# First weights in two DMAs, wider matmuls for tiles 2 and 3, interleaved statistics, and 1/den by one DMA, in a linear-attention and GELU block on one core

## The chip, the cores and the metric

The kernel runs on one core of a Trainium2 chip. The metric is device time in microseconds (us), from repeated executions; the profile is one execution more. In the profile PE is TensorE, PEld its weight loads, DVE VectorE, ACT ScalarE, POOL GpSimd, SP the engine that issues most DMAs. L352 is line 352 of the kernel; since the change adds lines, L352 of before is L355 of after, and L615 is L622.

A rounded map of the run: 0 to 7 us loading and the first normalised tile; 7 to 60 us `h = gelu(xn W1)`; 60 to 127 us the attention projections; 127 to 205 us the output products, with the division by the attention's denominator on the way.

## The reference, cut to what matters

```python
xn = (x - mean) / sqrt(var + 1e-5)                 # x is 2048 x 640, bf16
q, k, v = split(xn @ wqkv)                         # 32 heads of 20
pq, pk = phi(q), phi(k)
num = pq @ (pk.T @ v)                              # per head
den = pq @ sum(pk) + 1e-6
out = x + (num / den) @ wo + (gelu(xn @ w1 + b1) @ w2 + b2)   # w1: 640 x 1536
```

## The kernel before

Tokens come in 16 tiles of 128; 640 is five blocks k of 128, and W1's 1536 columns are 12 column blocks (`JT`) of 128, loaded as four quarters of three blocks (`JQ` = 3). All DMAs but two are issued from SP, in this order.

```python
dma_x(0, 1)
dma_w("scalar", b1tmp[:], ...)            # issued from ScalarE
dma_w1(0, "scalar")                       # W1's first quarter, 480 KB, issued from ScalarE
dma_x(1, 1)
dma_w1(1)
dma_x(2, 1)
dma_w1(2)
dma_x(3, 1)
dma_w1(3)
# ... x 4-5, 6-7, 8-11, 12-15; the other weights are queued behind the transposes
```

A helper records each operation with what it reads and writes, and puts in the semaphore waits. A filler is a warm-up matmul whose result nobody reads. One unit of `h` is five matmuls and a GELU on ScalarE:

```python
def h_unit(t0, n, jb):                    # n tiles from t0, column block jb
    # five matmuls: W1[:, k, block jb] against xnT[:, k, n*128 tokens], then GELU + bias on ScalarE
def ln_next(t):
    if t + 1 < NT:
        ln_half(t + 1, 0)                 # half the statistics of the next tile, VectorE
        ln_half(t + 1, 1)
    ln_norm(t)                            # VectorE; waits for rstd(t) from GpSimd
    if t + 1 < NT:
        ln_aggr(t + 1)                    # VectorE aggregate, then GpSimd power -> rstd = 1/sqrt(var + eps)

filler(10)                                # warm-up matmuls, 512 wide
# ... tile 0 normalised in two parts, transposed on TensorE, copied to xnT
h_first([0, 1, 2])                        # tile 0, first quarter: k 0,1 for three blocks, then k 2..4
xnT_copy(1, transp(1))
ln_stats(2)
ln_next(2)
units(0, 1, 3, 2 * JQ)                    # tile 0, second quarter
units(1, 1, 0, 2 * JQ)
units(0, 2, 2 * JQ, 2 * JQ + 2)           # tiles 0 and 1 together, 256 wide
xnT_copy(2, transp(2))
units(0, 2, 2 * JQ + 2, JT)
ln_next(3)
ln_next(4)
units(2, 1, 0, JQ)
xnT_copy(3, transp(3))
units(2, 1, JQ, JT)                       # tile 2 alone, 128 wide
units(3, 1, 0, JT)                        # tile 3 alone, 128 wide
for t in range(4, NT):                    # tiles 4..15 are transposed by DMA
    if t > 4:
        ln_next(t)
    # SP: dma_start_transpose(xnT[:, :, tile t], xn_tm[:, t, :])
for (t0, n) in [(4, 2), (6, 2), (8, 4), (12, 4)]:
    units(t0, n, 0, JT)
```

The division: 1/den is 32 rows (heads) for a chunk of 512 tokens; four DMAs spread it to 128 partitions, and VectorE multiplies it into `PQ`.

```python
def rden_dma(c):
    for i in range(4):
        # SP: dma_start(rdb(c)[i:P:4, :], rden[H * c:H * (c + 1), :])
```

Of the kernel before, what the change touches and what calls it, by code (L numbers as in the profile page):

```python
# [6 lines left out]
ACT = mybir.ActivationFunctionType  # L7
P = 128
# [104 lines left out]
def bass_parallel_sum__linear_attn_block__dense_activation_gelu__prompt_kernel(  # L113
# [6 lines left out]
    CW = CH * P  # L120
    NC = NT // CH
    DT = D // P
    JT = F // P
    H = 32
# [5 lines left out]
    Pl = Planner(nc)  # L130
    R_ = Pl.res
# [5 lines left out]
    with contextlib.ExitStack() as es:  # L137
# [12 lines left out]
        W1 = W1f[:].rearrange("p (k f) -> p k f", k=DT)  # L150
# [25 lines left out]
        rden = sb("rden", [P, CW], BF16)  # L176
# [3 lines left out]
        B_ = [R_("bank%d" % i) for i in range(8)]  # L180
# [22 lines left out]
        r_xn = [R_("xn%d" % t) for t in range(NT)]  # L203
        r_xnT = [R_("xnT%d" % t) for t in range(NT)]
        NW1 = 4
        r_W1 = [R_("W1_%d" % i) for i in range(NW1)]
        r_Wq, r_Wk, r_Wv, r_W2, r_Wo = R_("Wq"), R_("Wk"), R_("Wv"), R_("W2"), R_("Wo")
        r_b1tmp, r_b1c, r_b2 = R_("b1tmp"), R_("b1c"), R_("b2")
# [6 lines left out]
        r_PQ = [[R_("PQ%d_%d" % (c, j)) for j in range(DT)] for c in range(NC)]  # L215
# [5 lines left out]
        r_den, r_rden = R_("den"), R_("rden")  # L221
# [5 lines left out]
        def dma_x(t, n):  # L227
            src = xv[t * P:(t + n) * P, :].rearrange("(t p) d -> p t d", p=P)
            Pl.ins("sync", lambda e: e.dma_start(x_in[:, t:t + n, :], src),
                   writes=r_x[t:t + n], dma=True)  # L230

        def dma_w(eng, dst, src, res):
            Pl.ins(eng, lambda e: e.dma_start(dst, src), writes=[res], dma=True)  # L233

        w1v = B_w1.rearrange("(k p) n -> p k n", p=P)
        wqv = A_wqkv.rearrange("(k p) n -> p k n", p=P)
        FW = F // NW1
        def dma_w1(i, eng="sync"):
            dma_w(eng, W1[:, :, i * FW:(i + 1) * FW], w1v[:, :, i * FW:(i + 1) * FW], r_W1[i])
        dma_x(0, 1)  # L240
        dma_w("scalar", b1tmp[:], B_b1.rearrange("(a p) -> a p", p=P), r_b1tmp)
        dma_w1(0, "scalar")
        dma_x(1, 1)
        dma_w1(1)
        dma_x(2, 1)
        dma_w1(2)
        dma_x(3, 1)
        dma_w1(3)
        dma_x(4, 2)
        dma_x(6, 2)  # L250
        for c in range(2, NC):
# [10 lines left out]
        v = "vector"  # L262
# [7 lines left out]
               reads=[r_ident], writes=[r_ident])  # L270
# [22 lines left out]
        def filler(n):  # L293
            b = take(1)
            Pl.ins("tensor", [lambda e: e.matmul(bank(b), warm[:, 0:P], warm[:], start=True, stop=True)
                              for _ in range(n)], reads=[r_warm], writes=[B_[b]])

        def b1_step():
            b = take(1)
            Pl.ins("tensor", lambda e: e.transpose(bank(b).bitcast(BF16)[:, 0:JT], b1tmp[:], ident[:JT, :JT]),  # L300
                   reads=[r_b1tmp, r_ident], writes=[B_[b]])
            Pl.ins("scalar", lambda e: e.activation(b1c[:], bank(b).bitcast(BF16)[:, 0:JT], ACT.Copy),
                   reads=[B_[b]], writes=[r_b1c])


        def ln_half(t, h):
            s = t % 4
            Pl.ins(v, lambda e: e.bn_stats(stats[:, s, 6 * h:6 * h + 6], x_in[:, t, h * HW:(h + 1) * HW]),  # L308
                   reads=[r_x[t]], writes=[r_stats[s][h]])
            if h == 0:  # L310
                Pl.ins(g, lambda e: e.tensor_single_scalar(stats[:, s, 2:3], stats[:, s, 2:3], D * EPS, ALU.add),
                       reads=[r_stats[s][0]], writes=[r_stats[s][0]])

        def ln_aggr(t):
            s = t % 4
            Pl.ins(v, lambda e: e.bn_aggr(aggr[:, s, :], stats[:, s, :]),  # L316
                   reads=r_stats[s], writes=[r_aggr[s]])
            Pl.ins(g, lambda e: e.tensor_tensor(out=rstd[:, s:s + 1], in0=aggr[:, s, 1:2],  # L318
                                                in1=mhalf[:], op=ALU.pow),
                   reads=[r_aggr[s], r_small], writes=[r_rstd[s]])  # L320

        def ln_stats(t):
            ln_half(t, 0)
            ln_half(t, 1)
            ln_aggr(t)

        def ln_norm(t):
            s = t % 4
            Pl.ins(v, lambda e: e.tensor_scalar(xn_tm[:, t, :], x_in[:, t, :], aggr[:, s, 0:1], rstd[:, s:s + 1],
                                                ALU.subtract, ALU.mult),  # L330
                   reads=[r_x[t], r_aggr[s], r_rstd[s]], writes=[r_xn[t]])
# [32 lines left out]
        def norm0(lo, hi, res):  # L364
            Pl.ins(v, lambda e: e.tensor_scalar(xn_tm[:, 0, lo:hi], x_in[:, 0, lo:hi], aggr[:, 0, 0:1], rstd[:, 0:1],
                                                ALU.subtract, ALU.mult),
                   reads=[r_x[0], r_aggr[0], r_rstd[0]], writes=[res, r_xn[0]])

        def transp0(k0, k1, res):
            b = take(1)  # L370
            pT = bank(b).bitcast(BF16)
            Pl.ins("tensor", [(lambda e, k=k: e.transpose(pT[:, (k - k0) * P:(k - k0 + 1) * P],
                                                          xn_tm[:, 0, k * P:(k + 1) * P], ident[:]))
                              for k in range(k0, k1)],
                   reads=[res, r_ident], writes=[B_[b]])
            return xnT[:, k0:k1, 0:P], pT[:, 0:(k1 - k0) * P].rearrange("p (k q) -> p k q", k=k1 - k0), b

        def h_first(jbs):
            bs = [take(1) for _ in jbs]
            for (ks, res) in (((0, 1), r_xnTA), ((2, 3, 4), r_xnT[0])):  # L380
                for jb, b in zip(jbs, bs):
                    Pl.ins("tensor", [(lambda e, k=k, jb=jb, b=b: e.matmul(  # L382
                        bank(b, 0, P), W1[:, k, jb * P:(jb + 1) * P], xnT[:, k, 0:P],
                        start=(k == 0), stop=(k == DT - 1))) for k in ks],
                        reads=[r_W1[jb * P // FW], res], writes=[B_[b]])
            for jb, b in zip(jbs, bs):
                Pl.ins("scalar", lambda e, jb=jb, b=b: e.activation(
                    HG[:, jb, 0:P], bank(b, 0, P), ACT.Gelu_apprx_tanh, bias=b1c[:, jb:jb + 1]),
                    reads=[B_[b], r_b1c], writes=[r_HG[0][jb]])

        r_xnTA = R_("xnT0A")
        Pl.ins("scalar", lambda e: e.activation(b1c[:, 0:1], warm[:, 0:1], ACT.Gelu_apprx_tanh),
               reads=[r_warm], writes=[r_b1c])
        filler(10)
        ln_stats(0)
        ln_half(1, 0)
        ln_half(1, 1)
        ln_aggr(1)
        norm0(0, CA, r_xnA)
        norm0(CA, D, r_xnB)  # L400
        dA, sA, bA = transp0(0, 2, r_xnA)
        filler(1)
        dB, sB, bB = transp0(2, DT, r_xnB)
        Pl.ins(v, lambda e: e.tensor_copy(dA, sA), reads=[B_[bA]], writes=[r_xnTA])
        Pl.ins("scalar", lambda e: e.activation(dB, sB, ACT.Copy), reads=[B_[bB]], writes=[r_xnT[0]])
        b1_step()
        ln_norm(1)
        h_first([0, 1, 2])

# [5 lines left out]
        def units(t0, n, lo, hi):  # L415
            for jb in range(lo, hi):
                h_unit(t0, n, jb)

        def ln_next(t):
            if t + 1 < NT:  # L420
                ln_half(t + 1, 0)
                ln_half(t + 1, 1)
            ln_norm(t)
            if t + 1 < NT:
                ln_aggr(t + 1)

        xnT_copy(1, transp(1))
        ln_stats(2)
        ln_next(2)
        units(0, 1, 3, 2 * JQ)  # L430
        units(1, 1, 0, 2 * JQ)
        units(0, 2, 2 * JQ, 2 * JQ + 2)
        xnT_copy(2, transp(2))
        units(0, 2, 2 * JQ + 2, JT)
        ln_next(3)
        ln_next(4)
        units(2, 1, 0, JQ)
        xnT_copy(3, transp(3))
        units(2, 1, JQ, JT)
        units(3, 1, 0, JT)  # L440
        for t in range(TD, NT):
            if t > TD:
                ln_next(t)
# [128 lines left out]
        def rden_scale(c):  # L572
            cc = slice(c * CW, (c + 1) * CW)
            for j in range(DT):
                Pl.ins(v, lambda e, j=j: e.tensor_tensor(out=PQ[:, j, cc], in0=PQ[:, j, cc], in1=rdb(c), op=ALU.mult),
                       reads=r_rdb[c] + [r_PQ[c][j]], writes=[r_PQ[c][j]])

        ekf = ek[:].rearrange("p a d -> p (a d)")
        r_rdb = [[R_("rdb%d_%d" % (c, i)) for i in range(4)] for c in range(NC)]

        def rdb(c):
            return ekf[:, c % 3 * CW:(c % 3 + 1) * CW]

        def rden_dma(c):
            for i in range(4):
                Pl.ins("sync", lambda e, i=i: e.dma_start(rdb(c)[i:P:4, :], rden[H * c:H * (c + 1), :]),
                       reads=[r_rden], writes=[r_rdb[c][i]] + ([r_rdb[0][i]] if c == 3 else []), dma=True)

        def x_again(c):
            src = xv[c * CW:(c + 1) * CW, :].rearrange("(t p) d -> p t d", p=P)  # L590
# [133 lines left out]
```

## Time and profile before

| | before |
|---|---|
| time, median of 3 runs | 208.4 us (207.85 to 208.42) |
| span of the profiled execution | 206.8 us |
| TensorE busy | 98% |
| first real matmul | 6.87 us |
| fourth column block of tile 0 | 8.04 us |

The page's first line, its busy shares and its chain of what ended last:

```profile
span 206.8 us, 3962 instructions
...
PE 203.2 (98%) x1588; PEld 140.3 (68%) x1588; DVE 112.3 (54%) x231; ACT 73.1 (35%) x141; POOL 21.1 (10%) x59
...
PE 96%; DMA 3%; ACTq 0%; DVE 0%; issue 0%
```

The chain in order of time (start, length, what):

```profile
1.45 5.37 DMA W<-in_B_w_dram
6.82 0.05 issue
6.87 1.01 PE ps L382 x15
7.88 0.28 PE ps L336 x5
8.16 3.65 PE ps L352 x55
...
60.35 21.73 PE ps L473 x160
```

One DMA (W1's first quarter) holds the start back; then TensorE works to the end. So a change pays only by starting this stream sooner or by making it shorter. (The chain uses modelled ends of matmuls; L352's first matmul starts at 8.04.)

Two rows of the timeline, from the answers for 0 to 22 and 22 to 42 us (start, length, engine, line, operation, shape, count):

```profile
15.33 6.90 PE L352 MATMUL ps<-xnT,W 128*128 128x128 bf16 x113
...
21.74 20.49 PE L352 MATMUL ps<-xnT,W 128*128 128x256 bf16 x151
```

A row merges neighbours of one line and tile and shows the shape of the first. The program has 105 matmuls of 128 columns there, not 113, so the first row ends inside the 256-wide ones, and the second's start is only the edge of the window asked for. I overlooked that; narrower windows, asked after the result, show one shape each:

```profile
15.83 4.35 PE L352 MATMUL ps<-xnT,W 128*128 128x128 bf16 x75
...
22.83 10.43 PE L352 MATMUL ps<-xnT,W 128*128 128x256 bf16 x94
```

Taking off the last matmul's own length (0.219 and 0.273 us), that is (4.35 - 0.219)/74 = 55.8 ns a matmul at 128 columns and (10.43 - 0.273)/93 = 109.2 ns at 256.

VectorE's wait for 1/den in the list of waits (total, times, longest):

```profile
DVE PQ L575 <- DMA ek<-rden: 3.9, 1, 3.9
```

It is long, but no TensorE wait stands beside it: TensorE has products that need no division until 143.88 us.

### The profile page before, as it was taken

The page shows a single profiled execution, that of the slowest core. Times are in us where ns is not written, and L with a number is a line of the kernel's source. Part 1 is how long each engine was busy: PE and PEld are TensorE (multiplying, and loading weights), DVE is VectorE, ACT ScalarE, POOL GpSimd, SP SyncE. Part 2 cuts the span into 40 slices and gives each one's busy share as a digit, 9 for nine tenths or more (in the row PEclk, how much of TensorE's full clock was granted, in tenths as well). Part 3 has the DMA queues.
Part 4 walks back from the last instruction along what each step waited for, and adds up shares of the span by engine and source line. Part 5 has one row for each costly group of instructions (what it writes and reads, how often), then busy time and mean ns, then how long its engine had stood idle before and what let it go on. Part 6 is the DMA issues. An engine that isn't in the chain of part 4 may idle for free.

```text
span 206.8 us, 3962 instructions
## 1 busy us (share of the span) xinstructions
PE 203.2 (98%) x1588; PEld 140.3 (68%) x1588; DVE 112.3 (54%) x231; ACT 73.1 (35%) x141; POOL 21.1 (10%) x59
## 2 busy tenths in 40 slices
PE   7999999999999999999999999999999999999996
PEld 2799987444457777777756556677777777777775
DVE  4589970000007888999288888574863522522332
ACT  2689887666676555111153554400000000000000
POOL 3235568000022000000000000000000000000000
DMA  5999668998000000000300001931111111001002
GB/s 173 338 355 116 105 128 108 376 318 310 3 0 0 0 0 3 0 3 0 63 0 5 0 0 25 373 117 50 64 66 57 56 47 56 32 32 36 32 32 63
DMA packets 24043, 18.32 MB, mean 89 GB/s; under 512 B 10584, under 2 KB 24024, under 8 KB 24024
## 3 DMA queue, kind: packets, MB, share of 16 engines
q1 hardware_dynamic: 23344, 17.57, 29.8%
q10 hardware_dynamic: 680, 0.49, 0.9%
q8 instruction: 12, 0.20, 0.4%
q14 instruction: 7, 0.06, 0.1%
HBM read 12.62 MB, written 2.62 MB: 74 GB/s over the span
## 4 chain that ended last, share of the span: by engine, by line
PE 96%; DMA 3%; ACTq 0%; DVE 0%; issue 0%
PE ps L615 34%; PE ps L352 25%; PE ps L473 11%; PE ps L512 11%; PE ps L524 10%; DMA W<-in_B_w_dram 3%; PE ps L651 2%; PE ps L551 1%; PE ps L533 1%; PE ps L562 1%; PE ps L382 0%; PE ps L336 0%; ACTq L233 0%; DVE out_sb L654 0%
## 5 line engine op out<-in xcount | busy, mean ns | idle before, releaser
L352 PE MATMUL ps<-xnT,W 128*128 128x128 bf16 (+2 forms) x435 | 52.0, 282 | 0.0
L615 PE MATMUL ps<-W,HG 128*128 128x320 bf16 x360 | 51.0, 299 | 0.0
L352 PEld LDWEIGHTS ps<-xnT,W 128*128 128x128 bf16 x435 | 35.5, 98 | 15.7
L615 PEld LDWEIGHTS ps<-W,HG 128*128 128x128 bf16 x360 | 35.1, 98 | 14.2 <-issue 0.4
L356 ACT ACTIVATE HG<-ps,b1c 128x128 bf16<-128x128 f32 (+2 forms) x87 | 40.0, 492 | 12.6 <-PE ps L352 10.4
L634 DVE TENSOR_TENSOR out_sb<-ps,xnT 128x640 bf16<-128x640 f32 x15 | 12.4, 825 | 33.8 <-PE ps L615 33.6
L460 ACT ACTIVATE ek<-ps 128x512 bf16<-128x512 f32 (+1 forms) x36 | 23.2, 644 | 20.3 <-PE ps L524 11.1
L461 DVE TENSOR_SCALAR ek<-ek 128x512 bf16<-128x512 bf16 (+1 forms) x36 | 10.9, 304 | 33.7 <-ACT ek L460 32.6
L615 PE MATMUL ps<-Msb,PQ 128*128 128x320 bf16 x150 | 22.3, 299 | 0.0
L524 PE MATMUL ps<-xnT,Wqkv 128*128 128x512 bf16 x100 | 21.9, 379 | 0.0
L473 PE MATMUL ps<-Wqkv,xnT 128*128 128x320 bf16 x160 | 21.9, 299 | 0.0
L512 PE MATMUL ps<-xPK,xn_tm 128*128 128x320 bf16 x160 | 21.9, 299 | 0.0
L473 PEld LDWEIGHTS ps<-Wqkv,xnT 128*128 128x128 bf16 x160 | 15.7, 98 | 6.2
L512 PEld LDWEIGHTS ps<-xPK,xn_tm 128*128 128x128 bf16 x160 | 15.7, 98 | 6.1
L615 PEld LDWEIGHTS ps<-Msb,PQ 128*128 128x128 bf16 x150 | 14.7, 98 | 5.7
L524 PEld LDWEIGHTS ps<-xnT,Wqkv 128*128 128x128 bf16 x100 | 11.7, 118 | 9.5
L308 DVE BATCH_NORM_STATS2 stats<-xPK 128x6 f32<-128x320 bf16 x32 | 13.6, 466 | 2.8 <-DMA xPK<-in_A_x_dram 2.7
L463 DVE SCALAR_TENSOR_TENSOR PQ<-ps,ek 128x512 bf16<-128x512 f32 x20 | 13.8, 692 | 2.1
L463 DVE SCALAR_TENSOR_TENSOR xPK<-ps,ek 128x640 bf16<-128x640 f32 x16 | 13.2, 825 | 1.7
L499 DVE TENSOR_TENSOR Msb<-Msb,xPK 128x640 f32<-128x640 f32 x14 | 11.6, 825 | 0.5
L318 POOL TENSOR_TENSOR rstd<-aggr,mhalf 128x1 f32<-128x1 f32 x16 | 9.1, 568 | 8.9 <-DVE aggr L316 8.9
L516 ACT ACTIVATE W<-ps 128x640 bf16<-128x640 f32 x5 | 3.5, 703 | 18.2 <-PE ps L512 18.2
(61 smaller groups left out, 93.4 us busy)
## 6 DMA issues: line engine op xcount, KB each, us to landing
xnT<-in_A_x_dram SPq DMA_DIRECT2D x4, 640.0 KB, 6.8
Wqkv<-in_A_wqkv_dram SPq DMA_DIRECT2D x3, 800.0 KB, 6.9
out_dram<-out_sb SPq DMA_DIRECT2D x15, 160.0 KB, 1.8
W<-in_B_w_dram SPq DMA_DIRECT2D x1, 1920.0 KB, 15.4
W<-in_B_w_dram SPq DMA_DIRECT2D x3, 480.0 KB, 7.2
xPK<-in_A_x_dram SPq DMA_DIRECT2D x2, 640.0 KB, 8.6
Wo<-in_A_wo_dram SPq DMA_DIRECT2D x1, 800.0 KB, 10.8
xPK<-in_A_x_dram SPq DMA_DIRECT2D x4, 160.0 KB, 4.3
```

Of the source, the lines that this page charges most:

```text
L308: Pl.ins(v, lambda e: e.bn_stats(stats[:, s, 6 * h:6 * h + 6], x_in[:, t, h * HW:(h + 1) * HW]), reads=[r_x[t]], writes=[r_stats[s][h]])
L352: Pl.ins("tensor", [(lambda e, k=k: e.matmul(bank(b, 0, w), W1[:, k, jb * P:(jb + 1) * P], xnT[:, k, tok], start=(k == 0), stop=(k == DT - ...
L356: Pl.ins("scalar", lambda e: e.activation(HG[:, jb, tok], bank(b, 0, w), ACT.Gelu_apprx_tanh, bias=b1c[:, jb:jb + 1]), reads=[B_[b], r_b1c ...
L460: Pl.ins("scalar", lambda e: e.activation(e2, src, ACT.Exp), reads=br, writes=[r_ek[s]])
L461: Pl.ins(v, lambda e: e.tensor_scalar(et, et, 1.0, 1e-6, ALU.min, ALU.add), reads=[r_ek[s]], writes=[r_ek[s]])
L463: Pl.ins(v, lambda e: e.scalar_tensor_tensor(out=d2, in0=src, scalar=0.0, in1=e2, op0=ALU.max, op1=ALU.add), reads=br + [r_ek[s]], writes= ...
L473: fns.append(lambda e, k=k, h=h, b=b, t=t: e.matmul(bank(b + h, 0, HW), xnT[:, k, t * P:(t + 1) * P], Wqkv[:, k, D + h * HW:D + (h + 1) * ...
L499: Pl.ins(v, lambda e, t=t: e.tensor_tensor(out=zsum, in0=zsum, in1=PK[:, t, :], op=ALU.add), reads=[r_PK[t], r_zsum], writes=[r_zsum])
L512: Pl.ins("tensor", [(lambda e, t=t, h=h, b=b, f=f: e.matmul(bank(b + h, 0, HW), xn_tm[:, t, f * P:(f + 1) * P], PK[:, t, h * HW:(h + 1) * ...
L524: Pl.ins("tensor", [(lambda e, k=k, j=j, b=b: e.matmul(bank(b), Wqkv[:, k, j:D:DT], xnT[:, k, cc], start=(k == 0), stop=(k == DT - 1))) fo ...
L615: return lambda e: e.matmul(bank(b + h, 0, HW), l, r[:, h * HW:(h + 1) * HW], start=(i == 0), stop=(i == JT + DT - 1))
L634: Pl.ins(v, lambda e: e.tensor_tensor(out=halves(out_sb[:, s, :]), in0=pair(b), in1=halves(x_res[:, t, :]), op=ALU.add), reads=B_[b:b + 2] ...
```

## The change

The intent: W1's first quarter comes by two DMAs on two queues, so that tile 0 can begin with k blocks 0 and 1; tile 0's norm goes ahead of tile 1's aggregate; tiles 2 and 3 share the second half of W1 at 256 wide; only half of the next tile's statistics precedes each norm; 1/den takes one DMA a chunk, its source repeated four times.

```diff
+        KA = 2
         dma_x(0, 1)
         dma_w("scalar", b1tmp[:], ...)
-        dma_w1(0, "scalar")
+        dma_w("scalar", W1[:, 0:KA, 0:FW], w1v[:, 0:KA, 0:FW], r_W1A)
         dma_x(1, 1)
+        dma_w("sync", W1[:, KA:DT, 0:FW], w1v[:, KA:DT, 0:FW], r_W1[0])
         dma_w1(1)
+        dma_w1(2)
         dma_x(2, 1)
-        dma_w1(2)
+        dma_w1(3)
         dma_x(3, 1)
-        dma_w1(3)
@@ start
-        filler(10)
+        filler(6)
+        b1_step()
+        filler(3)
         ln_stats(0)
         ln_half(1, 0)
         ln_half(1, 1)
-        ln_aggr(1)
         norm0(0, CA, r_xnA)
         norm0(CA, D, r_xnB)
+        ln_aggr(1)
   (the two copies of tile 0's transposes change places: part A on ScalarE, part B on VectorE)
@@ ln_next
                 ln_half(t + 1, 0)
-                ln_half(t + 1, 1)
             ln_norm(t)
             if t + 1 < NT:
+                ln_half(t + 1, 1)
                 ln_aggr(t + 1)
@@ order of the units
         xnT_copy(1, transp(1))
-        ln_stats(2)
-        ln_next(2)
         units(0, 1, 3, 2 * JQ)
         units(1, 1, 0, 2 * JQ)
-        units(0, 2, 2 * JQ, 2 * JQ + 2)
+        units(0, 2, 2 * JQ, 3 * JQ)
+        ln_stats(2)
+        ln_norm(2)
+        ln_stats(3)
+        units(0, 2, 3 * JQ, 3 * JQ + 1)
         xnT_copy(2, transp(2))
-        units(0, 2, 2 * JQ + 2, JT)
+        units(0, 2, 3 * JQ + 1, JT)
         ln_next(3)
-        ln_next(4)
         units(2, 1, 0, JQ)
         xnT_copy(3, transp(3))
-        units(2, 1, JQ, JT)
-        units(3, 1, 0, JT)
+        units(2, 1, JQ, 2 * JQ)
+        ln_next(4)
+        units(3, 1, 0, 2 * JQ)
+        units(2, 2, 2 * JQ, JT)
@@ 1/den
-            for i in range(4):
-                dma_start(rdb(c)[i:P:4, :], rden[H * c:H * (c + 1), :])
+            src = rden[H * c:H * (c + 1), :].unsqueeze(1).to_broadcast([H, 4, CW])
+            dma_start(rdb(c), src)
```

More of the change, by code (lines that the diff above doesn't have):

```diff
@@ L205, in bass_parallel_sum__linear_attn_block__dense_activation_gelu__prompt_kernel @@
         NW1 = 4
+        r_W1A = R_("W1_0A")
         r_W1 = [R_("W1_%d" % i) for i in range(NW1)]
@@ L384, in h_first @@
                         start=(k == 0), stop=(k == DT - 1))) for k in ks],
-                        reads=[r_W1[jb * P // FW], res], writes=[B_[b]])
+                        reads=[r_W1A if res is r_xnTA else r_W1[jb * P // FW], res], writes=[B_[b]])
             for jb, b in zip(jbs, bs):
@@ L403, in bass_parallel_sum__linear_attn_block__dense_activation_gelu__prompt_kernel @@
         dB, sB, bB = transp0(2, DT, r_xnB)
-        Pl.ins(v, lambda e: e.tensor_copy(dA, sA), reads=[B_[bA]], writes=[r_xnTA])
-        Pl.ins("scalar", lambda e: e.activation(dB, sB, ACT.Copy), reads=[B_[bB]], writes=[r_xnT[0]])
-        b1_step()
+        Pl.ins("scalar", lambda e: e.activation(dA, sA, ACT.Copy), reads=[B_[bA]], writes=[r_xnTA])
+        Pl.ins(v, lambda e: e.tensor_copy(dB, sB), reads=[B_[bB]], writes=[r_xnT[0]])
         ln_norm(1)
@@ L575, in rden_scale @@
                 Pl.ins(v, lambda e, j=j: e.tensor_tensor(out=PQ[:, j, cc], in0=PQ[:, j, cc], in1=rdb(c), op=ALU.mult),
-                       reads=r_rdb[c] + [r_PQ[c][j]], writes=[r_PQ[c][j]])
+                       reads=[r_rdb[c], r_PQ[c][j]], writes=[r_PQ[c][j]])
         ekf = ek[:].rearrange("p a d -> p (a d)")
-        r_rdb = [[R_("rdb%d_%d" % (c, i)) for i in range(4)] for c in range(NC)]
+        r_rdb = [R_("rdb%d" % c) for c in range(NC)]
         def rdb(c):
@@ L584, in rden_dma @@
         def rden_dma(c):
-            for i in range(4):
-                Pl.ins("sync", lambda e, i=i: e.dma_start(rdb(c)[i:P:4, :], rden[H * c:H * (c + 1), :]),
-                       reads=[r_rden], writes=[r_rdb[c][i]] + ([r_rdb[0][i]] if c == 3 else []), dma=True)
+            src = rden[H * c:H * (c + 1), :].unsqueeze(1).to_broadcast([H, 4, CW])
+            Pl.ins("sync", lambda e: e.dma_start(rdb(c), src),
+                   reads=[r_rden], writes=[r_rdb[c]] + ([r_rdb[0]] if c == 3 else []), dma=True)
         def x_again(c):
```

## The prediction

> **What bounds the kernel now.** The page gives TensorE 98% busy over a 206.8 us span; the chain of waits that ended last is 96% TensorE and 3% DMA. The DMA piece is W1's first quarter: issued 1.45 us, landed 6.82; the first 15 real matmuls start at 6.87. From there to 204.95 the chain is TensorE without a gap.
>
> **What the change does, costed from the trace.**
>
> 1. Tiles 2 and 3, second half of W1: 60 matmuls 128 wide become 30 of 256. The timeline shows 105 of 128 columns from 15.49 to 21.74 us (59.5 ns each) and 120 of 256 from 21.74 to about 34.6 (107 ns each). Saved: 60 x 59.5 - 30 x 107 = 0.36 us, all on the critical path.
>
> 2. W1's first quarter in two parts. By packet counts in the DMA view the first 192 KB lands at about 4.7 us, the rest near 6. Tile 0's norm becomes the first limit: rstd ends at 5.07, and the norm no longer waits for tile 1's aggregate (5.42 to about 5.18). Then transposes, ScalarE's copy (about 0.4 us, from 0.49 for 384 columns), VectorE's copy: first matmuls at about 6.25, ending about 7.35 instead of 7.88.
>
> 3. The next gate stops most of that. W1's second quarter, issued 1.72, took 6.3 us: it landed at 8.02, and its matmuls started at 8.04. The same bytes must still move ahead of it; the skill's "DMA: Bandwidth & Descriptors", section "Issuing engines are not separate DMA queues", says a second queue saves only sequencer time, and the DMA share is about 100% from 4 us on. I expect it at 7.7 to 8.1, TensorE idle 0.2 to 0.5 us before it, and a net gain of 0.1 to 0.3 us.
>
> 4. Half statistics: x2 lands about 1.5 us later (W1's third quarter goes ahead); tile 2's norm then ends at about 12.2 against a need at 12.9. In the steady loop one half (0.42 us) is left to hide rstd's latency (aggregate start to norm 0.96 us), so its period grows from 1.32 to about 1.75 us a tile. Tile 5's DMA transpose then lands at about 21.3, just when tiles 4 and 5 are wanted (about 21.4). Cost: 0 to 0.4 us.
>
> 5. 1/den by one DMA a chunk: VectorE waits 3.9 us for it and scales at 142.18, but TensorE has unscaled products until 143.88 and never waits. Three issues of 0.6 us go; landing moves to about 140.5. Worth nothing.
>
> **Sum.** -0.36 - 0.2 + 0.05 = about -0.5 us: 207.9 us. Eight in ten: 207.2 to 208.5. Before's three runs span 0.57 us. Faster by over 2%: 1%. Within 2%: 98.5%. Slower: 0.5%.
>
> **What the profile would show.** First real matmul at about 6.25 without a DMA wait; a wait for W1 before the fourth column block, at about 8.0; 60 fewer 128-wide matmuls, 30 more 256-wide; tiles 4 and 5's matmuls at about 21.3 rather than 21.74; late norms 1.75 us apart, the last at about 36 rather than 30; VectorE's wait for 1/den down to about 2 us; everything after 60 us the same, shifted.
>
> **What would make it wrong.** W1's second quarter landing clearly earlier (gain up to 0.9 us), or later[...]; tile 5's transpose late (TensorE idle before tiles 4 and 5); TensorE's clock, cold for the ten fillers (0.43 us each), warming later with the shorter filler run.

## More of the kernel before

The granted TensorE clock was 1.0 in all but three runs: two of the kernel before (210.12 and 210.41 us) at 0.992, and one of e6 at 0.999. The two of before raise its mean in the calls of e5 to e8 and of e9 to e12, so that the ratios there lean towards the edits and their intervals are wide.

## The result, and the profile after

| | before | after |
|---|---|---|
| time, median of 6 runs | 208.29 us (207.85 to 208.42) | 208.31 us (208.03 to 208.65) |
| ratio, 95% interval | | 1.0004 (0.9990 to 1.0018) |
| span of the profiled execution | 206.8 us | 207.0 us |
| first real matmul | 6.87 us | 6.38 us |
| W1's second quarter landed | 7.99 us | 8.17 us |
| fourth column block of tile 0 | 8.04 us | 8.21 us |
| tiles 4 and 5, first matmul | 21.19 us | 21.43 us |
| first matmul of the projections | 60.19 us | 60.43 us |

A ratio is the mean time of one kernel's runs over that of the other's runs of the same rounds, so it is not quite the ratio of the medians quoted. The landings and single matmul starts are read one by one from the trace.

The time did not change. The prediction's range held, but the gain of 0.5 us in it did not come.

```profile
span 207.0 us, 3868 instructions
...
PE 202.8 (98%) x1557; PEld 139.5 (67%) x1557; DVE 113.7 (55%) x231; ACT 72.7 (35%) x135; POOL 21.5 (10%) x59
...
PE 95%; DMA 3%; SPq 1%; issue 0%; DVE 0%
```

TensorE has 31 matmuls and 31 weight loads fewer (30 by widening, one warm-up). The chain of after:

```profile
2.20 5.96 DMA W<-in_B_w_dram
8.17 0.05 issue
8.21 4.87 PE ps L355 x65
...
15.57 5.79 PE ps L355 x75
21.36 0.07 issue
21.43 39.16 PE ps L355 x240
60.59 21.73 PE ps L480 x160
```

The DMA in the chain is now W1's *second* quarter. By single matmul starts the fourth block begins 0.17 us later than before (8.04 to 8.21). What the earlier first matmuls gained is a hole in front of it, named by the waits between 7 and 9 us:

```profile
PE ps L355 <- DMA W<-in_B_w_dram: 0.4, 1, 0.4
```

The second new interruption is at 21.36: "issue" there is a wait that the profile gives to nobody. The trace has 0.346 us between two matmul starts that are 0.109 apart elsewhere, so 0.24 us are lost, and the next matmul is the first of tiles 4 and 5. Tile 5's transpose, asked for alone:

```profile
L451 SPq DMA_TRANSPOSE xnT<-xn_tm x1: 1199/1199/1199, 18.8 to 18.8; - x1
...
DMA to landing us min/median/max: 2.5/2.5/2.5
```

It was issued at 18.80 and landed at 21.34; TensorE went on at 21.43. In before the same transpose was issued at 17.19 and landed at 19.76, ahead of the need at 21.19:

```profile
L444 SPq DMA_TRANSPOSE xnT<-xn_tm x1: 1203/1203/1203, 17.2 to 17.2; - x1
...
DMA to landing us min/median/max: 2.6/2.6/2.6
```

The sum of the two profiles: +0.17 (fourth block), then -0.17 from there to the end of tile 3 (before 21.19 - 8.04 = 13.15 us, after 21.19 - 8.21 = 12.98), then +0.24 (tile 5): +0.24, which is 60.43 - 60.19. The -0.17 holds 60 x 55.8 - 30 x 109.15 = 0.07 us of widening; before's wait of 0.08 us ahead of tile 2's transposes is gone too. Two profiles are two executions, though, and the timed runs are equal; how much a single one may wander is seen below.

VectorE's wait for 1/den fell, to 2.8 us where about 2 was predicted, with nothing in the chain changed there (66.12 us from 134 to 200 us in both):

```profile
DVE PQ L582 <- DMA ek<-rden: 2.8, 1, 2.8
```

### The profile page after: what moved, and what is told of

It is laid out like the page before. It is cut to its first block, busy times and chain, and to the rows that moved or that the text cites. A ratio compares the mean times of both kernels' runs of the same rounds, so it can differ in the third digit from the quotient of the medians. Undisturbed runs are those within 1.5% of the kernel's fastest.

```text
span 207.0 us, 3868 instructions
## 1 busy us (share of the span) xinstructions
PE 202.8 (98%) x1557; PEld 139.5 (67%) x1557; DVE 113.7 (55%) x231; ACT 72.7 (35%) x135; POOL 21.5 (10%) x59
## 4 chain that ended last, share of the span: by engine, by line
PE 95%; DMA 3%; SPq 1%; issue 0%; DVE 0%
PE ps L622 34%; PE ps L355 25%; PE ps L519 10%; PE ps L480 10%; PE ps L531 10%; DMA W<-in_B_w_dram 3%; PE ps L658 2%; PE ps L558 1%; PE ps L540 1%; PE ps L569 1%; SPq L230 0%; PE ps L339 0%; SPq L234 0%; DVE out_sb L661 0%
## 5 line engine op out<-in xcount | busy, mean ns | idle before, releaser
L355 PE MATMUL ps<-xnT,W 128*128 128x256 bf16 (+2 forms) x405 | 52.1, 290 | 0.5 <-DMA W<-in_B_w_dram 0.4
L359 ACT ACTIVATE HG<-ps,b1c 128x256 bf16<-128x256 f32 (+2 forms) x81 | 39.6, 510 | 13.7 <-PE ps L355 11.3
L467 ACT ACTIVATE ek<-ps 128x512 bf16<-128x512 f32 (+1 forms) x36 | 23.2, 645 | 20.3 <-PE ps L531 10.6
L311 DVE BATCH_NORM_STATS2 stats<-xPK 128x6 f32<-128x320 bf16 x32 | 14.7, 470 | 3.8 <-DMA xPK<-in_A_x_dram 3.8
```

Source lines behind the costliest of these rows:

```text
L311: Pl.ins(v, lambda e: e.bn_stats(stats[:, s, 6 * h:6 * h + 6], x_in[:, t, h * HW:(h + 1) * HW]), reads=[r_x[t]], writes=[r_stats[s][h]])
L355: Pl.ins("tensor", [(lambda e, k=k: e.matmul(bank(b, 0, w), W1[:, k, jb * P:(jb + 1) * P], xnT[:, k, tok], start=(k == 0), stop=(k == DT - ...
L359: Pl.ins("scalar", lambda e: e.activation(HG[:, jb, tok], bank(b, 0, w), ACT.Gelu_apprx_tanh, bias=b1c[:, jb:jb + 1]), reads=[B_[b], r_b1c ...
L467: Pl.ins("scalar", lambda e: e.activation(e2, src, ACT.Exp), reads=br, writes=[r_ek[s]])
```

## The experiments

My theory after the result: (1) widening is worth 0.07 us, not 0.36; (2) the start is held by W1's second quarter; (3) tile 5's transpose holds what is left; (4) 1/den is worth nothing. Rivals are named with each run. Below, a gate is an arrival that TensorE has to wait for: W1's second quarter is the first, tile 5's transpose the second. Four kernels went in five rounds, and "before" is the kernel before in the same rounds.

### e1_den: before with 1/den by one DMA alone

The edit is the last hunk of the change alone.

> The kernel before with nothing but 1/den by one DMA a chunk. My theory: worth nothing, ratio 0.999 to 1.001, because VectorE's wait for 1/den (3.9 us before, 2.8 us after) is hidden behind TensorE's unscaled products; no TensorE wait near 144 us in either. Rival (this part is a gain or a loss that the other parts cancel): ratio below 0.999 or above 1.001, and the TensorE chain from 134 us to the end changes length.

Measured: 208.16 us median (208.06 to 208.41), before 208.17; ratio 0.9999 (0.9987 to 1.0011). No TensorE wait near 144 us. Alone, this part is worth nothing.

### e2_wide: before with the 256-wide matmuls alone

```diff
-        units(2, 1, JQ, JT)
-        units(3, 1, 0, JT)
+        units(2, 1, JQ, 2 * JQ)
+        units(3, 1, 0, 2 * JQ)
+        units(2, 2, 2 * JQ, JT)
```

> The kernel before with nothing but the second half of W1 for tiles 2 and 3 done 256 wide. Steps of the matmul starts in the trace are 55.8 ns at 128 columns and 109.15 ns at 256, so my theory now says 60 x 55.8 - 30 x 109.15 = 0.07 us gained, not the 0.36 us of the prediction: tiles 4 and 5's first matmul at about 21.12 us instead of 21.19, no new wait, ratio about 0.9997. Rival (the prediction's rates were right and something else ate it): that matmul at about 20.85, ratio about 0.998.

Measured: 208.93 us median (208.44 to 209.37), before 208.17; ratio 1.0037 (1.0025 to 1.0049). Both theories missed: fewer TensorE nanoseconds and a slower kernel. The loss is far from the edit. The waits between 143 and 147 us:

```profile
DVE PQ L576 <- DMA ek<-rden: 5.3, 1, 5.3
PEld ps L616 <- DVE PQ L576: 1.2, 5, 0.3
```

VectorE waits 5.3 us for 1/den instead of 3.9, and TensorE now waits for VectorE, five times, about 0.4 us in all by its matmul starts. The fourth of the first four 1/den DMAs, issued at 140.15, landed at 143.41; in before it was issued at 140.18 and landed at 142.06. What is new beside it is one packet of 16,384 bytes on a DMA queue that the profile calls "instruction", at 141.1 us for 1.09 us. In before that packet came at 137.5 (in e1, with the same TensorE instructions, at 138.6: its place wanders by about 1 us).

The Trainium skill, "Runtime: NRT & Kernel Launch", section "Instruction fetch mechanics", says that an engine's instructions are streamed in 16 KiB blocks of 256 instructions. The trace agrees: the packets are 16,384 bytes, and from 137.5 to 189.3 us the stretches between them hold 252, 254 and 256 TensorE instructions (matmuls and weight loads). So taking 60 TensorE instructions away moves every later fetch; at the output products' 0.136 us a matmul, 30 matmuls are 4.1 us, and the fetch moved by 3.6. That gave a new theory: the fetch now falls upon the 1/den DMAs. It is tested by e9, e10 and e11.

### e3_start: before with the new start alone

The hunks for the DMA order and the start, with before's order of statistics, units and 1/den.

> The kernel before with the start of the kernel after alone (W1's first quarter in two DMAs, the new order of DMAs, fillers, norms and copies up to the first 15 matmuls), the rest as before. My theory: W1's second quarter lands at about 8.17 us instead of 7.99, so the fourth column block starts about 0.17 us later than before (8.21 for 8.04) although the first 15 matmuls start 0.5 us earlier; x2 lands at about 10.1, x3 at about 12.0 and, with both tiles' statistics ahead of tile 2's norm as in the kernel before, tile 2's transposes are then late: TensorE idle some 1 us before them. Ratio 1.002 to 1.007. Rival (the start is a gain and the loss lies later): fourth block at 7.7 or earlier.

Measured: 209.73 us median (209.48 to 210.03), before 208.17; ratio 1.0074 (1.0062 to 1.0086). W1's second quarter landed at 8.23 and the fourth block started at 8.28; x3 landed at 12.10 and TensorE idled 1.52 us before tile 2's transposes, more than the 1 us expected. The start is no gain without the later order of the norms that goes with it. Tile 5's transpose was issued at 18.86 here, though the statistics come in before's order (17.19 in before, 18.80 in after).

### e4_both_halves: after with both halves ahead of each norm

```diff
                 ln_half(t + 1, 0)
+                ln_half(t + 1, 1)
             ln_norm(t)
             if t + 1 < NT:
-                ln_half(t + 1, 1)
                 ln_aggr(t + 1)
```

> The kernel after with both halves of the next tile's statistics ahead of each norm again. Late norms should be 1.32 us apart instead of 1.92. My theory: tile 5's aggregate comes at the same time as in the kernel after (about 17.35 us; the order of the norm and the second half before it does not matter to it), so its transpose still lands at about 21.3 us and the wait of about 0.24 us at tiles 4 and 5 stays, or moves to tile 3's transposes, which come 0.4 us later: time within 0.2 us of the kernel after. Rival (the longer period of the half statistics is what makes tile 5 late): that wait goes, L355's tiles 4 and 5 start at about 21.19, and the time falls by 0.24 us.

Measured: 208.07 us median (207.58 to 208.40), before 208.17; ratio 0.9991 (0.9979 to 1.0003), against 1.0004 (0.9990 to 1.0018) of the kernel after: the intervals overlap. The late transposes are issued 1.32 us apart again. The wait before tiles 4 and 5 is still there, 0.14 us. In this profile tile 5 landed at 20.65, which neither theory had, but so did everything sooner: W1's second quarter at 7.34 and x2 at 9.43, where after's profile has 8.17 and 10.11. The DMAs up to there are the same in both kernels. So the wandering of one execution is as large as the effects in question, and the half statistics are not shown to cost or gain anything.

### e5_no_gate: after without the second quarter's wait

```diff
         def h_unit(t0, n, jb):
+            wj = jb - 3 if (t0, n) == (0, 1) else jb
-                bank(b, 0, w), W1[:, k, jb * P:(jb + 1) * P], xnT[:, k, tok],
+                bank(b, 0, w), W1[:, k, wj * P:(wj + 1) * P], xnT[:, k, tok],
```

(and the same in what it reads.) It multiplies 3 of 12 column blocks of one tile by the wrong weights; the comparison's tolerance did not notice, but it is wrong by construction.

> The kernel after, wrong on purpose: column blocks 3 to 5 of tile 0 are multiplied with W1's first quarter instead of the second, so nothing asks for the second quarter at 7.6 us. My theory: the hole of 0.56 us before the fourth block (7.66 to 8.21) closes, the fourth block starts at about 7.66 and the later wait for the second quarter is over by then (asked at about 9.3). Of the 0.55 us, some comes back: tile 2's transposes are ready only at about 12.55 and tile 5's only at about 21.3 at the latest, so 0 to 0.4 us of the total is kept at the most. If tiles 4 and 5 still start at about 21.4, the second gate alone sets the time there. Rival (the hole is not the second quarter's landing but TensorE or its queue): the hole stays.

Measured: 208.29 us median (207.67 to 208.77), before 208.33; ratio 0.9984 (0.9952 to 1.0015). The hole closed: the fourth block started at 7.58, W1's second quarter landing at 8.16. Of those 0.63 us, 0.30 came back as a wait before tile 2's transposes (x2 had landed at 10.10), 0.08 as one for their copy, and the wait for tile 5 grew from 0.24 to 0.37: landed at 21.3, tile 5 let tiles 4 and 5 start at 21.34 instead of 21.43. So the theory holds: with the first gate gone, the second sets the time, and the whole head start is worth 0.09 us in the profile.

### e6_tile4_first: after with tile 4's first block ahead of tile 5

```diff
-        for (t0, n) in [(4, 2), (6, 2), (8, 4), (12, 4)]:
+        units(4, 1, 0, 1)
+        units(4, 2, 1, JT)
+        units(5, 1, 0, 1)
+        for (t0, n) in [(6, 2), (8, 4), (12, 4)]:
             units(t0, n, 0, JT)
```

> The kernel after, but the first column block of tiles 4 and 5 is done 128 wide, tile 4 first, tile 5 last, so TensorE has 0.28 us of work that does not need tile 5. My theory: the wait of 0.24 us at 21.2 us goes, at a price of 0.01 us; 0.22 us faster than the kernel after, ratio to before about 1.0000 less 0.001. Rival: that wait is not tile 5's transpose but tile 4's or an issue limit of TensorE; then it stays.

Measured: 208.67 us median (208.13 to 209.95), before 208.33 with a wide spread (207.81 to 210.12); ratio 1.0009 (0.9973 to 1.0045). The wait before tiles 4 and 5 is gone, so it was tile 5's. The time did not fall. In the profile the last stretch, from the last VectorE instruction to the end, took 2.25 us where it takes 1.51 in before and after; the last store took 2.20 us (205.43 to 207.63) instead of 1.45. In the trace an 8 KB packet on a second queue called "instruction" (q14) falls inside this store, at 206.49. The same happens in e8's profile (packet at 207.95, store from 207.06 to 209.31), and in the twelve others no such packet falls inside the last store and it took 1.43 to 1.45. So these 0.75 us probably come from that fetch and not from the order of the tiles; this was not tried, and the time of this run stays inconclusive.

### e7_split_q2: after with W1's second quarter in two DMAs as well

```diff
-        dma_w1(1)
+        dma_w("sync", W1[:, 0:KA, FW:2 * FW], w1v[:, 0:KA, FW:2 * FW], r_W1B)
+        dma_w("sync", W1[:, KA:DT, FW:2 * FW], w1v[:, KA:DT, FW:2 * FW], r_W1[1])
@@
-        units(0, 1, 3, 2 * JQ)
+        h_first([3, 4, 5])
```

> The kernel after, with W1's second quarter also in two DMAs (k blocks 0 and 1, then 2 to 4) and tile 0's column blocks 3 to 5 done as the first three are: k 0 and 1 for all three, then the rest. My theory: the first part lands at about 7.0 us, 6 matmuls (0.33 us) fill the hole from 7.66, the remaining 9 start at about 8.2 to 8.3, so the point after tile 0's blocks 3 to 5 comes 0.2 to 0.33 us earlier; of that, tile 5's transpose at 21.3 keeps nothing: the wait there grows from 0.24 to about 0.5 us and the time stays as in the kernel after.

Measured: 208.06 us median (207.93 to 208.79), before 208.33; ratio 0.9980 (0.9949 to 1.0011). The parts landed at 6.61 and 7.45, the hole was gone, and TensorE waited 0.26 us before tiles 4 and 5 (expected 0.5), because tile 5 landed at 21.0. The interval includes 1.

### e8_both: e6 and e7 together

> Both mends: W1's second quarter in two DMAs, and tile 4's first block ahead. My theory: gains add up to what tile 5's landing allows, with 0.28 us of cover: about 0.4 to 0.5 us below the kernel after, 206.5 to 206.6 us of span, ratio to before about 0.998, faster than both kernels. If the TensorE wait for tile 5 is still there, it is what is left.

Measured: 210.22 us median (208.43 to 210.94), before 208.33; ratio 1.0064 (1.0020 to 1.0108). The opposite of what was expected; five of six runs are above 209.8. The chain between 18 and 24 us:

```profile
18.94 4.23 DMA xnT<-xn_tm
23.17 0.05 issue
```

Tile 5's transpose took 4.23 us instead of 2.5, and TensorE waited about 1.7 us for it, cover or no cover. (Two smaller losses stand beside it in this profile: the second part of W1's second quarter landed at 8.40, which left a hole of 0.53 us, and the last store took 0.8 us more, as in e6.) The DMA view from 18 to 24 us (40 slices of 0.15 us, DMA busy in tenths, then GB/s):

```profile
DMA  0069999400000069999500000007999890000001
GB/s 0 0 140 229 218 213 203 88 2 0 0 0 0 0 135 218 218 215 312 100 3 0 0 0 0 0 10 162 227 222 191 85 246 4 0 0 0 0 0 29
...
q8 instruction: 1, 0.02, 1.2%
```

The first burst is tile 4's transpose, the second tile 5's, and the slice with 312 GB/s holds the 16 KB instruction fetch, at 20.8 us for 1.1 us: it began in the middle of the burst. After's fetch came at 22.8 us, in tile 6's transpose, which took 4.1 us and was not wanted before 28. In each of the ten profiles so far at least one transpose in flight at the fetch between 19.7 and 22.8 us took 3.9 us or more. With e6's edit the fetch came earlier both times (21.2 for 22.8 us in e6 against after, 20.8 for 22.6 in e8 against e7), and here it fell on the one transpose that TensorE was waiting for. (Why it came earlier is not shown, and that the fetch causes the delay is an inference here; e11 tests the same thing at 1/den.)

### e9_after_four_dmas: after with 1/den by four DMAs

The last hunk of the change undone.

> The kernel after with 1/den by four DMAs a chunk again. The profiles show TensorE's instruction fetches as 16 KB packets on a DMA queue of their own, 256 TensorE instructions apart; with 60 fewer TensorE instructions (30 matmuls and their weight loads) the fetch near 137.5 us moved to 141 to 142, into the time of the 1/den DMAs. My theory: with four DMAs (issues to about 142.3) the fetch catches the last of the first four, the scale starts after 143.5 and TensorE waits at 144, 0.2 to 0.6 us in all: ratio 1.002 to 1.005 to the kernel before, where the kernel after had 1.0004. Rival (1/den is worth nothing, as predicted): 1.000, no wait near 144 us.

Measured: 209.02 us median (208.46 to 209.65), before 208.15 (207.84 to 208.97 and one of 210.41); ratio 1.0030 (0.9989 to 1.0071), the wide interval owed to that one run. The waits between 143 and 147 us:

```profile
DVE PQ L582 <- DMA ek<-rden: 5.9, 1, 5.9
PEld ps L622 <- DVE PQ L582: 1.8, 5, 0.9
PE ps L622 <- DVE PQ L582: 0.6, 1, 0.6
```

and the chain around it:

```profile
140.07 3.84 DMA ek<-rden
...
144.03 0.43 DVE PQ L582
144.47 0.05 issue
144.52 1.65 PE ps L622 x9
```

The fetch came at 141.3 for 1.4 us, and the fourth 1/den DMA took 3.84 us instead of 1.9. TensorE restarted at 144.52 after a gap of 0.74 us and then went at VectorE's pace for four blocks, about 0.25 us more. By medians, and against the kernel after in another call (208.31), the one DMA is worth some 0.7 us *in the kernel after*, though nothing in the kernel before.

### e10_wide_den: before with the 256-wide matmuls and one DMA

> The kernel before with the 256-wide matmuls and 1/den by one DMA a chunk. My theory: the 0.40 us of TensorE waits near 144 us that the 256-wide matmuls alone brought (e2_wide, 1.0037) are gone, since the single DMA lands at about 141, before or with the fetch; ratio 0.9990 to 1.0005. Rival (the 256-wide matmuls cost the time in another way): stays at 1.003 or more.

Measured: 208.14 us median (207.82 to 208.35), before 208.15; ratio 0.9983 (0.9949 to 1.0017). All six runs are below the lowest of e2_wide (208.44). The two DMAs of the first two chunks were issued at 138.7 and 139.4 and landed at 141.32 and 142.05, no later than the fetch at 142.05; no TensorE wait near 144 us.

### e11_wide_pad: e2_wide with the instruction count put back

```diff
-        filler(10)
+        filler(40, P)          # 40 warm-up matmuls of 128 columns for 10 of 512
```

> The kernel before with the 256-wide matmuls and four DMAs a chunk, but the ten opening warm-up matmuls of 512 columns cut into 40 of 128: 30 more matmuls and weight loads, where TensorE has nothing else to do, so the instruction count at 130 us is that of the kernel before. My theory (the place of the fetch makes the wait): the fetch is back at about 137.5 us, the first four 1/den DMAs land by 142.1, no wait at 144 us, ratio 0.999 to 1.001 although 1/den still takes four DMAs. Rival (anything else in the 256-wide matmuls makes it): 1.003 or more, wait at 144 us.

Measured: 208.09 us median (207.84 to 208.44), before 208.15; ratio 0.9982 (0.9948 to 1.0016). 1/den still takes four DMAs, and the matmuls are e2_wide's; only 30 matmuls and weight loads were added in the warm-up, 130 us earlier. The fetch was back at 137.6 us, the fourth DMA landed at 142.5, and there was no TensorE wait near 144 us. All six runs are at or below e2_wide's lowest. That settles it: the place of the instruction fetch made e2_wide's loss. The chain has no wait from 134.57 us on:

```profile
134.57 66.12 PE ps L616 x486
```

### e12_best: the causes mended together

```diff
   (e7's edit, and in the order of the DMAs:)
-        dma_w1(2)
-        dma_x(2, 1)
-        dma_w1(3)
-        dma_x(3, 1)
+        dma_x(2, 1)
+        dma_w1(2)
+        dma_x(3, 1)
+        dma_w1(3)
   (e4's edit, and:)
         units(2, 1, 0, JQ)
+        ln_half(5, 0)
+        ln_half(5, 1)
         xnT_copy(3, transp(3))
+        ln_norm(4)
+        ln_aggr(5)
         units(2, 1, JQ, 2 * JQ)
-        ln_next(4)
```

> The kernel after with the causes mended: W1's second quarter in two DMAs, x2 and x3 ahead of W1's third and fourth quarters as in the kernel before, tile 3 to 5's statistics earlier and both halves ahead of each norm from there on. My theory: blocks 3 to 5 of tile 0 done 0.2 to 0.6 us sooner than in the kernel before, tile 5's transpose lands at about 20.1 us, out of reach of the fetch at 21 to 23, no TensorE wait before tiles 4 and 5, which start at 20.5 to 20.9 us (21.19 before, 21.43 after): 0.3 to 0.7 us below the kernel before, ratio 0.9965 to 0.9985. Rival: another DMA wait takes its place, ratio 0.999 or more.

Measured: 207.83 us median (207.44 to 207.97), before 208.15 (207.84 to 210.41); ratio 0.9968 (0.9934 to 1.0001). The chain has no DMA after x0:

```profile
6.40 1.11 PE ps L386 x15
...
15.17 44.90 PE ps L356 x315
```

Tile 5's transpose landed at 20.3 and was not waited for; the fetch, at 21.4, fell on later ones, with slack. The projections begin at 59.90 us (60.19 before, 60.43 after). By the medians it is 0.32 us better than before and 0.48 better than the after of another call; the interval just includes no gain. Before's run of 210.41 us counts in it; without that run the means are 207.79 and 208.21. It is the best version that ran, by a margin at the edge of what five rounds can show.

## Why the prediction was right or wrong, point by point

The range (207.2 to 208.5) and "within 2%" were right. The gain of 0.5 us was not there; two terms were mis-sized and one step was wrong. That the range held is in part luck: the widening's loss of about 0.8 us and the one DMA that removes it were both unforeseen, and they cancelled.

1. **"Saved: 60 x 59.5 - 30 x 107 = 0.36 us": the size failed.** The rates came from merged timeline rows. One shape at a time gives 55.8 and 109.15 ns, so 0.07 us. The Trainium skill, "TensorE: Matmul & The Clock Gate", section "Wait — 56ns, not 53.3ns?", gives, once the array is warm, N columns over 2.4 GHz plus about 2.5 ns: an estimate by that rule is 55.8 ns at 128 and 109.2 at 256. The trace agrees to a tenth of a nanosecond; checking the read rate against it would have caught the error. Widening from 128 to 256 saves only one such constant each time; the weight loads it also saves were hidden already.

2. **"First matmuls at about 6.25": right in kind** (6.38 in after; 6.35 to 6.50 in the profiles with this start).

3. **"The next gate stops most of that ... a net gain of 0.1 to 0.3 us": mechanism right, size wrong.** The hole and its cause came as described (e5). The second quarter landed at 8.17, past the 7.7 to 8.1 expected, and the net was -0.17 us in that pair of profiles. But with the same DMA order it landed at 8.17, 8.23, 7.34, 8.16, 8.29 and 7.71 us (after, e3, e4, e5, e6, e9). A gain of 0.1 to 0.3 cannot be told from that wandering, nor from the timed runs. The skill's "DMA: Bandwidth & Descriptors", section "Issuing engines are not separate DMA queues", on which the step rested (a second queue saves only sequencer time), fits what was seen: the first 192 KB landed sooner (4.3 to 5.4 us), the quarter behind them did not come reliably sooner.

4. **"Tile 5's DMA transpose then lands at about 21.3, just when tiles 4 and 5 are wanted ... cost: 0 to 0.4 us": right in place, entered too low in the sum** (0.05; measured 0.24). e5 shows that this gate alone decides once the first is open, so gains at the start and in the widening could not be added to each other: the sum itself was the wrong operation. Its stated cause was also off: the norms are 1.92 us apart instead of 1.75, but putting both halves back (e4) left the wait in place. What makes tile 5 late is the new start, whose DMA order lands x2 and x3 1.6 us later (10.11 and 12.05 us for 8.50 and 10.42): with it and before's statistics (e3) the transpose was issued 1.67 us later than in before, with it and the new statistics (after) 1.61. The prediction had named x2's delay and found it harmless for tile 2, but did not follow it to tile 5. e12, which puts x2 and x3 ahead again and also moves tile 5's statistics, has no wait (which of the two counts there was not tried apart).

5. **"1/den by one DMA a chunk ... worth nothing": wrong as a part of this change.** Alone it is worth nothing (e1). But the widening takes TensorE instructions away, which moves the instruction fetches; one then lands on the 1/den DMAs, and with four DMAs it costs TensorE about 0.4 us of waits in e2's profile and about 1 us in e9's, 0.8 us and 0.9 us by medians against before. One DMA finishes ahead of the fetch. The step that failed is "TensorE has unscaled products until 143.88 and never waits": that slack, 1.7 us, was read from one placement of the fetch. e11 shows the placement to be the cause.

So the expected gain went, in order: most of the widening's was never there; the start's went into the wait for W1's second quarter and then for tile 5; and the part "worth nothing" paid for a loss that the widening brought in 120 us after its own place.

## What to carry to other kernels

Size a saving from rows that hold one shape, and do not add gains that lie ahead of the same later gate: ask when the next thing to be waited for arrives. In a stream that is TensorE all the way, a changed instruction count moves the instruction fetches everywhere behind it, so look at which awaited DMA they fall on before blaming or crediting the edit. Where a chain of small DMAs has little slack, one DMA is safer than four even if the profile shows no wait today.

## What the Trainium skill lacked or had wrong

- "Runtime: NRT & Kernel Launch", "Instruction fetch mechanics", calls the cost of crossing a block boundary "mostly hidden". The size of a block is confirmed (16,384 bytes, 252 to 256 TensorE instructions apart from 137.5 us on). But beside a fetch of 0.9 to 1.6 us the kernel's own transfers took longer: a 32 KB DMA that lands in 1.9 us took 3.3 to 3.8 (e2, e9), a DMA transpose of 2.6 us took 3.5 to 4.9. The page does not warn of it, and in e8's profile TensorE lost 1.73 us where such a transpose was awaited.
- No page says that one and the same sequence of loads may land 0.9 us apart from execution to execution: 7.34 to 8.29 us for W1's second quarter, about 1.3 MB into the run.
- No page gives what a DMA transpose of 128 x 640 bf16 within the on-chip memory costs (a time for 128 x 128 and bandwidths are there, but no time for this size): 1.2 to 1.3 us of issue and 2.5 to 2.7 us to landing here, so that twelve of them keep the issuing engine busy for some 15 us.
- "TensorE: Matmul & The Clock Gate" is exact here: 55.8 ns at 128 and 109.15 ns at 256 columns, with a new weight load for each matmul.
